# Expert visits in two sizes: 18 of 256 rows and 51 of 384 instead of 65 of 384

## The chip, the core and the metric

The kernel runs on one core of a Trainium2 chip. The metric is the device time of one execution in microseconds (us), the median over several runs. The core's engines are PE (matrix multiply, with its weight loads, PEld), DVE (vector), ACT (scalar activation), POOL (GpSimd) and SP, which only issues DMAs here.

## The reference

Three stages follow one another on 8 x 3072 = 24576 rows of 256 numbers:

```python
X = np.fft.rfft(x, axis=1)                       # a filter in the frequency domain
x = np.fft.irfft(X * F, n=3072, axis=1).reshape(24576, 256)

expert_idx = argmax(normalised(x) @ normalised(expert_emb).T / tau)   # 8 experts
for e in range(8):                               # each row goes to one expert
    mask = expert_idx == e
    out[mask] = gate_w[mask, None] * (np.maximum(x[mask] @ w1[e], 0) @ w2[e])
    # w1[e]: 256 x 1024, w2[e]: 1024 x 256

h = x @ w_in                                     # w_in: 256 x 2048, given as float64
return (h - np.tanh(h)) @ w_out                  # w_out: 2048 x 256, float64
```

## The kernel before

**Three stages.** `fft_phase` transforms the rows, picks an expert for each and scatters the row (with its gate and its number) into that expert's part of `region` in DRAM. `Moe` then works through the experts in *visits*: a visit takes a fixed number of rows of one expert, multiplies by w1, applies relu, multiplies by w2 and stores the columns to `x2T`. `ff_phase` does the last stage on 48 tiles of 512 rows.

**Three products for one.** For accuracy each float32 operand is held as a high and a low part (`w1h`, `w1l`, `yh`, `yl`, `hh`, `hl`, `w2h`, `w2l`), and each product is three matmuls: high x high, high x low, low x high.

**Visits.** The first KV = 9 visits (256 rows each, TE) belong to one expert, chosen early, and run under the end of the first stage. After them stand 65 visits of TV = 384 rows. Their number is fixed when the kernel is built, so that it suffices for any split of the rows over the experts: 58 whole pieces and 7 that the experts' remainders may add. Which expert and which rows a visit takes is worked out on the chip, by `moe_schedule` (some 40 tiny DVE operations on one small table); SP reads expert, row and target column of each visit from this table. A visit beyond the last one that is needed does its work on columns that nobody reads. Visits go through the experts from the last to the first, so the weights change only where the expert does; the load of a visit's weights (`raw`, 4 DMAs of 512 KB, `wload`) is conditional on that. The splitting of weights into high and low parts (`split`) is done for every visit.

**The order inside a visit.** A visit has four steps, b2 = 0 to 3. The order in which each engine gets its work is written out by hand in the loop of `visits` (lines 882 to 908): in step (v, b2) come `up(v, b2)` (12 matmuls, L807), a quarter of the weight split of visit v + 1 (`w1l` on DVE in steps 0 and 1, `w2l` on POOL in steps 2 and 3, L757), one of three parts of preparing the rows of visit v + 1 (`scale` in step 0: `ys` on POOL L769, `it` on DVE L773; `turn` in step 1: transposes L778, L779; `parts` in step 2: `yh` on ACT, `yl` on DVE L786), `relu(v, b2)` (`hh` on ACT L817, `hl` on DVE L818), the load of the weights and, in step 2, of the rows of visit v + 2, then perhaps a piece of *side work*, and `down` of two steps earlier (12 matmuls, L835). At the end of a visit's last `down`, `finish` copies the output and takes its maximum (`mx`, DVE L846). So step (v, 1) holds the `mx` of visit v - 1.

**Side work.** `ff_weights` is a generator that turns the float64 weights of the last stage into float32 parts, on 32 blocks. Each block is three pieces of small integer operations on DVE: piece 1 (six operations, L469 to L474), piece 2 (four, L476 to L479), piece 3 (four, L481 to L485). `next(self.side)` emits one piece at its place in the order. Before, it is called in step 3 of every one of the 65 visits, and in step 1 of the first 36:

```python
if v >= KV and (b2 == 3 or b2 == 1 and v - KV < 100 - (NV - KV - 1)):   # L900
    next(self.side, None)
```

**Buffers.** `up` writes two PSUM tiles in a 384-row visit, from two pools that alternate by step; each pool has two tiles, so `up` of a step needs the `relu` of two steps earlier to be done.

Of the kernel before, what the change touches and what calls it, by code (L numbers as in the profile page):

```python
# [16 lines left out]
F32 = mybir.dt.float32  # L17
# [9 lines left out]
D = 256  # L27
# [92 lines left out]
def fft_phase(tc, K, x, fr, fn, fi, emb, tau, region, base, NB, CAP, moe):  # L120
# [3 lines left out]
    with ExitStack() as es:  # L124
# [51 lines left out]
        first = cp.tile([128, 8], F32, name="first")  # L176
        nc.vector.tensor_scalar(first, dec, -float(CAP), 8.0 * CAP + TV, op0=ALU.mult, op1=ALU.add)
        nc.vector.tensor_copy(base, first)
# [213 lines left out]
        def at(slot, f, *args):  # L392
            slots[slot].append(lambda: f(*args))
# [138 lines left out]

def moe_schedule(tc, cp, cnt, done, numbers, CAP, step):

    nc = tc.nc
    v = nc.vector
    A = lambda n: cp.tile([128, 8], F32, name=n)
# [8 lines left out]
    assert TV == 3 * 128 and CAP < 250 * 128  # L552
    v.tensor_scalar(t, left, 127.0, None, op0=ALU.add)
    v.tensor_copy(ti, t)
    v.tensor_scalar(ti, ti, 7, None, op0=ALU.logical_shift_right)
    v.tensor_copy(t, ti)
    v.tensor_scalar(t, t, 2.0, 171.0, op0=ALU.add, op1=ALU.mult)
    v.tensor_copy(ti, t)
    v.tensor_scalar(ti, ti, 9, None, op0=ALU.logical_shift_right)
    nv = A("scnv")  # L560
    v.tensor_copy(nv, ti)
    step()

    vin, sin = A("scvi"), A("scsi")
    v.tensor_tensor_scan(vin, ones, nv, 0.0, op0=ALU.mult, op1=ALU.add)
    v.tensor_tensor_scan(sin, ones, left, 0.0, op0=ALU.mult, op1=ALU.add)
    vis, e8 = numbers
# [4 lines left out]
    v.scalar_tensor_tensor(w, vis, -1.0, vin[:, 7:8], op0=ALU.mult, op1=ALU.add)  # L572
    v.tensor_scalar(wp, w, 0.0, None, op0=ALU.add)
    v.tensor_scalar(w, w, -1.0, None, op0=ALU.add)
# [9 lines left out]
    e, ep = expert(w, "a"), expert(wp, "b")  # L584
    step()
# [9 lines left out]
    ve, se, ne = pick(vin, "v"), pick(sin, "s"), pick(cnt, "n")  # L595
    step()

    j = col("scj")
    v.tensor_tensor(j, ve, w, op=ALU.subtract)
    v.tensor_scalar(j, j, -float(TV), None, op0=ALU.mult)  # L600
# [5 lines left out]
    v.scalar_tensor_tensor(row, row, float(TV), used, op0=ALU.add, op1=ALU.mult)  # L606
    v.tensor_tensor(dst, se, j, op=ALU.add)
    v.scalar_tensor_tensor(dst, dst, float(TV), used, op0=ALU.add, op1=ALU.mult)
    step()
    v.tensor_copy(res[:, 2:3], e)  # L610
    v.tensor_tensor(new, e, ep, op=ALU.not_equal)
    start = col("sclt")
    v.tensor_scalar(start, vis, 1.0, None, op0=ALU.is_lt)
    v.tensor_tensor(new, new, start, op=ALU.max)
    v.tensor_copy(resi, res)
    return resi


class Moe:
# [4 lines left out]


    def __init__(self, tc, gp, region, w1, w2, x2T, ids, N, CAP):
        self.tc, self.gp, self.region, self.w1, self.w2 = tc, gp, region, w1, w2
        self.x2T, self.ids, self.N, self.CAP = x2T, ids, N, CAP
        self.KV = (N - 2 * S) // (8 * TE)
        self.NV = self.KV + (N - self.KV * TE) // TV + 7  # L630
        self.mx = gp.tile([128, self.NV], F32, name="mx")
        self.sent, self.early = [], []
        self.sc = self.side = self.raw = None
        self.n = 0
        self.es = ExitStack()
# [74 lines left out]
    def visits(self):  # L710
        tc, region, x2T, ids, mx = self.tc, self.region, self.x2T, self.ids, self.mx
        N, CAP, KV, NV = self.N, self.CAP, self.KV, self.NV
# [77 lines left out]
        def up(v, b2):  # L790

            w1h, w1l = W[v][:2]
            yh, yl, _ = X[v]
            if v < KV:
                t = self.hp[0].tile([128, 2, TE], F32, name="h")
                h = [t[:, 0], t[:, 1]]
                H[v, b2] = [t]
            else:
                k = 4 * (v - KV) + b2
                h = [self.hp[k % 2].tile([128, 512], F32, name="h")[:, :TV] for j in range(2)]  # L800
                H[v, b2] = h
# [19 lines left out]
        def down(v, b2):  # L821
            w2h, w2l = W[v][2:]
            hh, hl = H.pop((v, b2))
            if b2 == 0:
                if v < KV:
                    t = self.op[0].tile([128, 512], F32, name="o")
                    O[v] = [t[:, :TE], t[:, TE:]]
                else:
                    O[v] = [self.op[(2 * (v - KV) + d + 1) % 4 > 0].tile([128, 512], F32, name="o")[:, :TV] for d in range(2)]
            for j in range(2):  # L830
                fb = 2 * b2 + j
                for d in range(2):
                    c = slice(128 * d, 128 * d + 128)
                    for n, (p, q) in enumerate(((w2h, hh), (w2h, hl), (w2l, hh))):
                        nc.tensor.matmul(O[v][d], p[:, fb, c], q[:, j], start=fb == 0 and n == 0 and (d == 0 or v >= KV),  # L835
                                         stop=fb == 7 and n == 2 and (d == 1 or v >= KV))
            if b2 == 3:
                finish(v)

        def finish(v):  # L840
# [41 lines left out]
        for k in range(len(steps) + LAG):  # L882
            if k < len(steps):
# [27 lines left out]
def ff_load(tc, pool, bufs, eng, x2T, ids, c):  # L911
# [7 lines left out]
    def load():  # L919
        return (eng.dma_start(x, x2T[:, TV:][:, c].rearrange("(k p) n -> p k n", p=128)),  # L920
                eng.dma_start(ix, ids[TV:][c].rearrange("(a p) -> p a", a=4)))

# [170 lines left out]
def build(tc, a, out, NB):  # L1093
    nc = tc.nc
    N = NB * S
    CAP = N + TV
    with ExitStack() as es:
# [4 lines left out]
        region = dp.tile([8 * CAP, 264], F32, name="region")  # L1102
        x2T = dp.tile([D, N + TV], F32, name="x2T")
        ids = dp.tile([N + TV], I32, name="ids")
        moe = Moe(tc, gp, region, a["w1"], a["w2"], x2T, ids, N, CAP)
        with tc.manual_schedule():
            fft_phase(tc, a, a["x"], a["fr"], a["fn"], a["fi"], a["emb"], a["tau"], region, cnt, NB, CAP, moe)
            sc = moe_schedule(tc, gp, cnt, moe.done, numbers, CAP, moe.step)
            wp = es.enter_context(tc.tile_pool(name="w", bufs=1, side="right"))
# [53 lines left out]
```

## Time and profile before

| | |
|---|---|
| median of 3 runs | 4018.46 us (4014.62 to 4025.91) |
| the profiled execution | 4024.83 us, span 4023.0 us |
| PE busy | 3904.8 us, 97% of the span |
| DVE, ACT, POOL busy | 65%, 62%, 51% |
| first matmul of the experts' stage, last | 590.7, 1815.6 us (its last `mx` at 1823.2) |
| granted clock of PE, mean | 0.99 |

The span runs from the first to the last instruction of the profiled execution. The first 590 us are the first stage, 733 to 1823 us the 65 visits, and what follows is the last stage. Busy shares are means over all of it; what counts for a stage is read in that stage.

### The profile page before, as it was taken

To read this page: it belongs to the slowest core of one execution; us is meant where nothing else is said; L and a number is where in the kernel's file an instruction comes from. 1 tells how busy PE (TensorE), PEld (TensorE's weight loads), DVE (VectorE), ACT (ScalarE), POOL (GpSimd) and SP (SyncE) were. 2 spreads that over 40 slices of the span, in tenths; PEclk is the share of its full clock that TensorE was granted. 3 is DMA by queue.
4 is the path that set the end of the run, shared out by engine and by line. 5 is a ranking of instruction groups with operands and counts; after the bars stand their busy time and mean duration, and the time that the engine had idled before them with its cause. 6 is when DMAs were issued, how large, how long until landed. Compare 5 with 4: busy or idle time off the path is not lost.

```text
span 4023.0 us, 65752 instructions
## 1 busy us (share of the span) xinstructions
PE 3904.8 (97%) x23204; PEld 3527.1 (88%) x23204; DVE 2621.8 (65%) x4370; ACT 2514.1 (62%) x4318; POOL 2051.7 (51%) x1514
## 2 busy tenths in 40 slices
PE   6899979999999999999999999999999999999998
PEld 3666659999999999999999999999999999999987
DVE  4799986788888877865555555555555555555554
ACT  3455544555555555556777777777777777777775
POOL 2366664344444444444555555555555555555545
PEclk8999999999999999999999999999999999999999
DMA  9898863332333232221000000000001000000000
GB/s 275 264 295 279 270 186 102 76 80 62 77 80 80 55 75 75 54 71 35 22 26 28 22 22 23 26 27 22 22 24 30 22 22 22 26 28 22 22 17 17
DMA packets 297874, 300.13 MB, mean 75 GB/s; under 512 B 158905, under 2 KB 240450, under 8 KB 297538
## 3 DMA queue, kind: packets, MB, share of 16 engines
q1 hardware_dynamic: 275714, 241.83, 21.3%
q0 software_dynamic: 18432, 51.14, 3.5%
q8 instruction: 184, 3.01, 0.3%
q10 hardware_dynamic: 3392, 2.90, 0.2%
q14 instruction: 152, 1.25, 0.1%
HBM read 282.46 MB, written 132.72 MB: 103 GB/s over the span
## 4 chain that ended last, share of the span: by engine, by line
PE 85%; DVE 7%; DMA 4%; issue 2%; POOL 1%; SPq 1%; ACT 1%; POOLq 0%; DVEq 0%; ACTq 0%
PE po L1034 27%; PE h L991 26%; PE h L807 14%; PE o L835 14%; DVE u L261 1%; DVE v L260 1%; DVE v L259 1%; DMA out<-ob,ix 1%; PE z L254 1%; PE z L269 1%; PE z L296 1%; PE L L308 1%; PE z L229 1%; DMA region<-Y,pi 1%; DMA z1d<-a 1%
## 5 line engine op out<-in xcount | busy, mean ns | idle before, releaser
L999 POOL TENSOR_TENSOR gl<-g,gh 128x512 fp32r<-128x512 f32 x768 | 992.9, 1293 | 987.7 <-ACT gh L998 980.4
L1008 DVE SCALAR_TENSOR_TENSOR s<-s,u 128x512 f32<-128x512 f32 x768 | 535.0, 697 | 951.9 <-ACT s L1007 950.1
L1034 PE MATMUL po<-wo,gh 128*128 128x256 f32 x6144 | 1143.0, 282 | 0.0
L1034 PEld LDWEIGHTS po<-wo,gh 128*128 128x128 f32 x6144 | 1007.3, 189 | 71.3
L1034 PE MATMUL po<-wo,gl 128*128 128x256 f32 x3072 | 874.7, 285 | 4.0 <-POOL gl L999 4.0
L1006 ACT ACTIVATE u<-h 128x512 f32<-128x512 f32 x768 | 459.0, 598 | 584.1 <-PE h L991 583.9
L991 PE MATMUL h<-xh,wih 128*128 128x512 f32 x1536 | 610.7, 398 | 0.1
L991 PE MATMUL h<-xl,wih 128*128 128x512 f32 x1536 | 607.6, 396 | 0.0
L991 PE MATMUL h<-xh,wil 128*128 128x512 f32 x1536 | 603.9, 393 | 0.0
L1034 PEld LDWEIGHTS po<-wo,gl 128*128 128x128 f32 x3072 | 581.2, 189 | 4.3 <-POOL gl L999 4.2
L1009 DVE TENSOR_TENSOR g<-s,h 128x512 f32<-128x512 f32 x768 | 529.1, 689 | 84.5 <-POOL gl L999 3.7
L1007 ACT ACTIVATE s<-u,beta 128x512 f32<-128x512 f32 x768 | 554.7, 722 | 25.2
L757 POOL TENSOR_TENSOR w2l<-raw,w2h 128x1024 fp32r<-128x1024 f32 x130 | 349.9, 2692 | 416.7 <-ACT w2h L756 414.4
L817 ACT ACTIVATE hh<-h 128x384 fp32r<-128x384 f32 (+1 forms) x556 | 269.5, 498 | 458.1 <-PE h L807 443.4
L998 ACT ACTIVATE gh<-g 128x512 fp32r<-128x512 f32 x768 | 485.4, 632 | 11.2 <-PE po L1034 4.9
L807 PE MATMUL h<-yh,w1h 128*128 128x384 f32 (+1 forms) x1184 | 392.4, 331 | 10.7 <-DVE hl L818 7.3
L807 PE MATMUL h<-yh,w1l 128*128 128x384 f32 (+1 forms) x1184 | 389.5, 329 | 2.4 <-DVE w1l L757 2.3
L807 PE MATMUL h<-yl,w1h 128*128 128x384 f32 (+1 forms) x1184 | 389.4, 329 | 0.1
L835 PE MATMUL o<-hh,w2h 128*128 128x384 f32 (+1 forms) x1184 | 388.4, 328 | 0.2 <-ACT x L845 0.2
L835 PE MATMUL o<-hl,w2h 128*128 128x384 f32 (+1 forms) x1184 | 388.2, 328 | 0.0
L835 PE MATMUL o<-hh,w2l 128*128 128x384 f32 (+1 forms) x1184 | 388.1, 328 | 0.0
L991 PEld LDWEIGHTS h<-xh,wil 128*128 128x128 f32 x1536 | 288.5, 188 | 71.0
(199 smaller groups left out, 6102.2 us busy)
## 6 DMA issues: line engine op xcount, KB each, us to landing
raw<-in_w SPq DMA_DIRECT2D x260, 512.0 KB
y<-region SPq DMA_DIRECT2D x260, 99.0 KB
x2T<-x SPq DMA_DIRECT2D x65, 384.0 KB
xt<-in_x SPq DMA_DIRECT2D x48, 512.0 KB
z1d<-a SPq DMA_DIRECT2D x96, 256.0 KB
A<-z1d SPq DMA_DIRECT2D x64, 384.0 KB
z3d<-b SPq DMA_DIRECT2D x128, 192.0 KB
bt<-z3d SPq DMA_DIRECT2D x96, 256.0 KB
```

The costliest lines, as they stand in the source:

```text
L757: eng.tensor_tensor(l, r, h.bitcast(F32), op=ALU.subtract)
L807: nc.tensor.matmul(h[j], p[:, k, c], q[:, k], start=n == 0, stop=n == 5)
L817: nc.scalar.activation(oh, t, AF.Relu)
L835: nc.tensor.matmul(O[v][d], p[:, fb, c], q[:, j], start=fb == 0 and n == 0 and (d == 0 or v >= KV), stop=fb == 7 and n == 2 and (d == 1 or ...
L991: nc.tensor.matmul(h, a[:, k, c], b[:, k], start=n == 0, stop=n == 5)
L998: nc.scalar.activation(gh, g, AF.Copy)
L999: nc.gpsimd.tensor_tensor(gl, g, gh.bitcast(F32), op=ALU.subtract)
L1006: nc.scalar.activation(u, h, AF.Square)
L1007: nc.scalar.activation(s, u, AF.Square, bias=beta)
L1008: nc.vector.scalar_tensor_tensor(s, s, KAPPA, u, op0=ALU.add, op1=ALU.mult)
L1009: nc.vector.tensor_tensor(g, s, h, op=ALU.mult)
L1034: nc.tensor.matmul(po[a // 2][:, a % 2], p[:, a], wo[:, f, q], start=f == 0 and n == 0 and a % 2 == 0, stop=f == 15 and n == 2 and a % 2 == 1)
```

## The change

The visits after the first nine come in two sizes. `moe_visits` sets their numbers: 9, then 18 of 256 rows, then 51 of 384 (for 24576 rows). `KF` = 27 is the first visit of 384. `moe_schedule` hands out whole pieces of 384 first, up to 51 in all, and lets the visits of 256 take what the experts then have left; the visits of 256 run first, from the last expert to the first, then the visits of 384 do the same again. In the first visit of each kind the weights are loaded in any case. The table costs 17 DVE operations more.

A visit of 256 rows is built like one of the first nine: one PSUM tile holds both halves of `up`, and `relu` is one operation on ACT and one on DVE for each step. It alternates between the two pools, so that four steps' tiles exist. Its weights are loaded and split like those of a visit of 384.

No side work is called in the visits of 256. In the visits of 384 it is called in steps 1 and 3, in step 2 too where v is no multiple of 3, and in all four steps of the first one. The spare columns and rows at the edges of `region` and `x2T` shrink from 384 to 256, so that 16 blocks of zeros are written instead of 24.

```diff
+def moe_visits(N):
+    first = (N - 2 * S) // (8 * TE)
+    rest = N - first * TE
+    full = -(-(rest - 8 * (TV - 1)) // TV)
+    return first, (rest - full * TV - 8) // TE + 8, full
...
-        self.KV = (N - 2 * S) // (8 * TE)
-        self.NV = self.KV + (N - self.KV * TE) // TV + 7
+        self.KV, few, full = moe_visits(N)
+        self.KF = self.KV + few
+        self.NV = self.KF + full
...
-        size = lambda v: TE if v < KV else TV
+        size = lambda v: TE if v < KF else TV
...
-            if v < KV:
-                t = self.hp[0].tile([128, 2, TE], F32, name="h")
+            k = 4 * (v - KV) + b2
+            if v < KF:
+                t = self.hp[k % 2 if v >= KV else 0].tile([128, 512], F32, name="h").rearrange("p (j n) -> p j n", j=2)
...
-                if v >= KV and (b2 == 3 or b2 == 1 and v - KV < 100 - (NV - KV - 1)):
+                if v >= KF and (b2 % 2 or v == KF or b2 == 2 and v % 3):
                     next(self.side, None)
...
 def moe_schedule(...):
+    vf, cut = A("scvf"), A("scct")
+    v.tensor_tensor_scan(vf, ones, nf, 0.0, op0=ALU.mult, op1=ALU.add)
+    v.tensor_scalar(vf, vf, float(NF), None, op0=ALU.min)
...
+    v.tensor_tensor(t, left, cut, op=ALU.subtract)
+    v.tensor_scalar(t, t, TE - 1.0, None, op0=ALU.add)
+    v.tensor_copy(ti, t)
+    v.tensor_scalar(ti, ti, 8, None, op0=ALU.logical_shift_right)
...
-        for i in range(TV // 128 * E):
-            at(31 + i, zeros, *divmod(128 * i, TV))
+        for i in range(TE // 128 * E):
+            at(31 + i, zeros, *divmod(128 * i, TE))
```

**Where the order moves.** The rows are an engine's instructions in program order: line, operation, output <- inputs, size.

DVE in the middle of a visit of 384, from step 2 of one visit to step 0 of the next; `cvm`, `cvl`, `cvr`, `cvf`, `wil` are the side work. Before:

```order
L786 TENSOR_TENSOR yl<-yt,yh 128x768
L818 SCALAR_TENSOR_TENSOR hl<-h,hh 128x384 x4
L476 TENSOR_SCALAR cvm<-cvs 128x256
L477 TENSOR_SCALAR cvl<-cvs 128x256
L478 TENSOR_TENSOR cvm<-cvm,cvl 128x256
L479 TENSOR_TENSOR cvf<-cva,cvm 128x256
L757 TENSOR_TENSOR w1l<-raw_5497,w1h 128x1024
```

The same place in the change, in a visit with side work in steps 1, 2 and 3:

```order
L823 TENSOR_TENSOR yl<-yt,yh 128x768
L855 SCALAR_TENSOR_TENSOR hl<-h,hh 128x384 x2
L476 TENSOR_SCALAR cvm<-cvs 128x256
L477 TENSOR_SCALAR cvl<-cvs 128x256
L478 TENSOR_TENSOR cvm<-cvm,cvl 128x256
L479 TENSOR_TENSOR cvf<-cva,cvm 128x256
L855 SCALAR_TENSOR_TENSOR hl<-h,hh 128x384 x2
L481 TENSOR_SCALAR cvl<-cvs 128x256
L482 SCALAR_TENSOR_TENSOR cvr<-cvl,cva 128x256
L484 TENSOR_TENSOR cvl<-cvf,wih 128x256
L485 TENSOR_TENSOR wil<-cvl,cvr 128x256
L794 TENSOR_TENSOR w1l<-raw_5489,w1h 128x1024
```

A second piece stands between the `hl` of step 2 and that of step 3; the one behind step 3 stays.

DVE in one visit after the first nine. Before, from the `mx` of a visit's step 1 to the `hl` of the next visit's step 0:

```order
L846 TENSOR_REDUCE mx<-x_7437 128x1
L786 TENSOR_TENSOR yl<-yt,yh 128x768
L818 SCALAR_TENSOR_TENSOR hl<-h,hh 128x384 x4
L469 TENSOR_SCALAR cva<-cvs 128x256
L470 TENSOR_SCALAR cva<-cva 128x256
L471 TENSOR_SCALAR cva<-cva 128x256
L472 TENSOR_SCALAR cva<-cva 128x256
L473 TENSOR_SCALAR cvm<-cvs 128x256
L474 TENSOR_TENSOR cva<-cva,cvm 128x256
L757 TENSOR_TENSOR w1l<-raw_5497,w1h 128x1024
L772 MEMSET it 32x32
L773 COPY it<-y 32x12
```

The same stretch of a visit of 256 in the change, and on to its next `hl`:

```order
L883 TENSOR_REDUCE mx<-x_7447 128x1
L823 TENSOR_TENSOR yl<-yt,yh 128x512
L855 SCALAR_TENSOR_TENSOR hl<-h,hh 128x2x256 x2
L794 TENSOR_TENSOR w1l<-raw_5489,w1h 128x1024
L809 MEMSET it 32x32
L810 COPY it<-y 32x8
L855 SCALAR_TENSOR_TENSOR hl<-h,hh 128x2x256
```

One `hl` stands where two stood, and there is no side work.

## Rows read from the trace of the kernel before

**Rows 1.** The page's chain of work that ended last, shares of the span by line.

```profile
PE po L1034 27%; PE h L991 26%; PE h L807 14%; PE o L835 14%; DVE u L261 1%; DVE v L260 1%; DVE v L259 1%; DMA out<-ob,ix 1%; PE z L254 1%; PE z L269 1%; PE z L296 1%; PE L L308 1%; PE z L229 1%; DMA region<-Y,pi 1%; DMA z1d<-a 1%
```

**Rows 2.** Windows of the experts' stage: length, then busy us (x instructions).

```profile
core 0: us, PE busy (x) PEld busy (x) DVE busy (x) ACT busy (x) POOL busy (x), PEclk, DMA share, GB/s
...
800.00:900.00 100.00, 98.21 (x567) 97.89 (x566) 87.50 (x150) 56.03 (x94) 44.62 (x18) 1.00 0.31 81
900.00:1000.00 100.00, 100.00 (x579) 100.00 (x578) 89.81 (x151) 56.75 (x95) 44.21 (x19) 1.00 0.23 60
...
1400.00:1500.00 100.00, 100.00 (x579) 100.00 (x578) 78.57 (x125) 56.10 (x92) 44.74 (x19) 1.00 0.31 76
```

**Rows 3.** The chain in order of time: start us, us, what; 690 to 760.

```profile
693.12 1.44 PE h L807 x12
...
741.01 2.08 PE h L807 x12
```

**Rows 4.** Timeline of DVE, one visit: start, us, line, operation, shapes [idle before <-releaser].

```profile
940.86 2.53 DVE L786 TENSOR_TENSOR yl<-yt,yh 128x768 fp32r<-128x768 f32 x1 [0.69 <-ACT yh L785]
943.31 1.68 DVE L818 SCALAR_TENSOR_TENSOR hl<-h,hh 128x384 fp32r<-128x384 f32 x3
...
945.89 0.28 DVE L469 TENSOR_SCALAR cva<-cvs 128x256 int32<-128x256 int32 x1
...
947.74 2.53 DVE L757 TENSOR_TENSOR w1l<-raw,w1h 128x1024 fp32r<-128x1024 f32 x1
...
951.35 1.20 DVE L757 TENSOR_TENSOR w1l<-raw,w1h 128x1024 fp32r<-128x1024 f32 x1
...
954.37 0.27 DVE L476 TENSOR_SCALAR cvm<-cvs 128x256 int32<-128x256 int32 x1
...
955.34 0.43 DVE L479 TENSOR_TENSOR cvf<-cva,cvm 128x256 int32<-128x256 int32 x1
...
957.50 2.54 DVE L786 TENSOR_TENSOR yl<-yt,yh 128x768 fp32r<-128x768 f32 x1 [0.73 <-ACT yh L785]
```

**Rows 5.** Timeline of POOL in the same visit.

```profile
940.17 5.48 POOL L757 TENSOR_TENSOR w2l<-raw,w2h 128x1024 fp32r<-128x1024 f32 x2 [7.04 <-ACT w2h L756]
947.71 1.47 POOL L769 TENSOR_TENSOR ys<-y 128x768 f32<-128x768 f32 x1 [2.06 <-DMA y<-region]
956.81 5.48 POOL L757 TENSOR_TENSOR w2l<-raw,w2h 128x1024 fp32r<-128x1024 f32 x2 [7.62 <-ACT w2h L756]
```

**Rows 6.** Timeline of DVE behind a reload of weights, 863 to 880.

```profile
866.22 0.16 DVE L773 COPY it<-y 32x12 int32<-32x12 int32 x1 [2.72 <-DMA y<-region]
...
871.70 2.37 DVE L469 TENSOR_SCALAR cva<-cvs 128x256 int32<-128x256 int32 x1
874.11 2.40 DVE L470 TENSOR_SCALAR cva<-cva 128x256 int32<-128x256 int32 x1
```

**Rows 7.** Timeline of POOL around the same reload.

```profile
854.88 5.48 POOL L757 TENSOR_TENSOR w2l<-raw,w2h 128x1024 fp32r<-128x1024 f32 x2 [6.51 <-ACT w2h L756]
867.85 1.93 POOL L769 TENSOR_TENSOR ys<-y 128x768 f32<-128x768 f32 x1 [7.48 <-DMA y<-region]
871.52 4.84 POOL L757 TENSOR_TENSOR w2l<-raw,w2h 128x1024 fp32r<-128x1024 f32 x2 [1.75 <-ACT w2h L756]
```

**Rows 8.** Timeline of PE, all matmuls from 735 us on with idle before.

```profile
880.08 0.44 PE L807 MATMUL h<-yh,w1h 128*128 128x384 f32 x1 [1.79 <-DVE hl L818]
...
1032.24 0.54 PE L807 MATMUL h<-yh,w1h 128*128 128x384 f32 x1 [2.10 <-DVE hl L818]
...
1168.23 0.44 PE L807 MATMUL h<-yh,w1h 128*128 128x384 f32 x1 [1.03 <-DVE hl L818]
...
1335.64 0.44 PE L807 MATMUL h<-yh,w1h 128*128 128x384 f32 x1 [0.72 <-DVE hl L818]
```

**Rows 9.** The chain in order of time, behind two of these stalls.

```profile
880.08 2.37 PE h L807 x12
...
1032.24 3.91 PE h L807 x12
```

**Rows 10.** Timeline of DVE: one operation of the schedule's table.

```profile
687.01 0.17 DVE L555 TENSOR_SCALAR scti<-scti 128x8 int32<-128x8 int32 x1
```

More of the change, by code (lines that the diff above doesn't have):

```diff
@@ L176, in fft_phase @@
         first = cp.tile([128, 8], F32, name="first")
-        nc.vector.tensor_scalar(first, dec, -float(CAP), 8.0 * CAP + TV, op0=ALU.mult, op1=ALU.add)
+        nc.vector.tensor_scalar(first, dec, -float(CAP), 8.0 * CAP + TE, op0=ALU.mult, op1=ALU.add)
         nc.vector.tensor_copy(base, first)
@@ L530, in moe_numbers, with moe_schedule @@
     return r
-def moe_schedule(tc, cp, cnt, done, numbers, CAP, step):
+def moe_visits(N):
[3 more added lines that the diff above has]
+    return first, (rest - full * TV - 8) // TE + 8, full
+def moe_schedule(tc, cp, cnt, done, numbers, N, CAP, step):
     nc = tc.nc
     v = nc.vector
+    _, NE, NF = moe_visits(N)
     A = lambda n: cp.tile([128, 8], F32, name=n)
@@ L550, in moe_schedule @@
     v.tensor_tensor(left, cnt, done, op=ALU.subtract)
-    assert TV == 3 * 128 and CAP < 250 * 128
-    v.tensor_scalar(t, left, 127.0, None, op0=ALU.add)
-    v.tensor_copy(ti, t)
+    vis, e8 = numbers
+    isf, is0 = col("scif"), col("sci0")
+    v.tensor_scalar(isf, vis, float(NE), None, op0=ALU.is_ge)
+    v.tensor_scalar(is0, vis, float(NE), None, op0=ALU.is_equal)
+    start = col("sclt")
+    v.tensor_scalar(start, vis, 1.0, is0, op0=ALU.is_lt, op1=ALU.add)
+    assert TV == 3 * 128 and TE == 2 * 128 and CAP < 250 * 128
+    v.tensor_copy(ti, left)
     v.tensor_scalar(ti, ti, 7, None, op0=ALU.logical_shift_right)
     v.tensor_copy(t, ti)
-    v.tensor_scalar(t, t, 2.0, 171.0, op0=ALU.add, op1=ALU.mult)
+    v.tensor_scalar(t, t, 171.0, None, op0=ALU.mult)
     v.tensor_copy(ti, t)
     v.tensor_scalar(ti, ti, 9, None, op0=ALU.logical_shift_right)
-    nv = A("scnv")
-    v.tensor_copy(nv, ti)
+    nf = A("scnf")
+    v.tensor_copy(nf, ti)
     step()
-    vin, sin = A("scvi"), A("scsi")
-    v.tensor_tensor_scan(vin, ones, nv, 0.0, op0=ALU.mult, op1=ALU.add)
+    vf, cut = A("scvf"), A("scct")
+    v.tensor_tensor_scan(vf, ones, nf, 0.0, op0=ALU.mult, op1=ALU.add)
+    v.tensor_scalar(vf, vf, float(NF), None, op0=ALU.min)
+    v.tensor_copy(cut, vf)
+    v.tensor_tensor(cut[:, 1:], vf[:, 1:], vf[:, :7], op=ALU.subtract)
+    v.tensor_scalar(cut, cut, float(TV), None, op0=ALU.mult)
+    v.tensor_tensor(t, left, cut, op=ALU.subtract)
+    v.tensor_scalar(t, t, TE - 1.0, None, op0=ALU.add)
+    v.tensor_copy(ti, t)
+    v.tensor_scalar(ti, ti, 8, None, op0=ALU.logical_shift_right)
+    v.tensor_copy(t, ti)
+    step()
+    vin, sin, ve_ = A("scvi"), A("scsi"), A("scve")
+    v.tensor_tensor_scan(ve_, ones, t, 0.0, op0=ALU.mult, op1=ALU.add)
     v.tensor_tensor_scan(sin, ones, left, 0.0, op0=ALU.mult, op1=ALU.add)
-    vis, e8 = numbers
+    v.tensor_tensor(t, vf, ve_, op=ALU.subtract)
+    v.scalar_tensor_tensor(vin, t, isf, ve_, op0=ALU.mult, op1=ALU.add)
     res = cp.tile([128, 4], F32, name="scres")
@@ L571, in moe_schedule @@
     w, wp = col("scw"), col("scwp")
[L572 to L574 removed]
+    v.scalar_tensor_tensor(wp, isf, float(NE), vis, op0=ALU.mult, op1=ALU.subtract)
+    v.tensor_tensor(wp, wp, vin[:, 7:8], op=ALU.add)
+    v.tensor_scalar(w, wp, -1.0, None, op0=ALU.add)
     def expert(x, nm):
@@ L584, in moe_schedule @@
     e, ep = expert(w, "a"), expert(wp, "b")
+    nend, send, nif = A("scne"), A("scse"), col("scni")
+    v.tensor_scalar(nif, isf, -1.0, None, op0=ALU.add)
+    v.scalar_tensor_tensor(nend, cut, nif, cnt, op0=ALU.mult, op1=ALU.add)
+    v.scalar_tensor_tensor(send, cut, nif, sin, op0=ALU.mult, op1=ALU.add)
     step()
@@ L593, in pick @@
         return r
-    ve, se, ne = pick(vin, "v"), pick(sin, "s"), pick(cnt, "n")
+    ve, se, ne = pick(vin, "v"), pick(send, "s"), pick(nend, "n")
     step()
-    j = col("scj")
+    j, size = col("scj"), col("scz")
     v.tensor_tensor(j, ve, w, op=ALU.subtract)
-    v.tensor_scalar(j, j, -float(TV), None, op0=ALU.mult)
+    v.tensor_scalar(size, isf, float(TE - TV), -float(TE), op0=ALU.mult, op1=ALU.add)
+    v.tensor_tensor(j, j, size, op=ALU.mult)
     used = col("scu")
@@ L605, in moe_schedule @@
     v.tensor_tensor(row, row, ne, op=ALU.add)
-    v.scalar_tensor_tensor(row, row, float(TV), used, op0=ALU.add, op1=ALU.mult)
+    v.scalar_tensor_tensor(row, row, float(TE), used, op0=ALU.add, op1=ALU.mult)
     v.tensor_tensor(dst, se, j, op=ALU.add)
-    v.scalar_tensor_tensor(dst, dst, float(TV), used, op0=ALU.add, op1=ALU.mult)
+    v.scalar_tensor_tensor(dst, dst, float(TE), used, op0=ALU.add, op1=ALU.mult)
     step()
@@ L824, in down @@
             if b2 == 0:
-                if v < KV:
-                    t = self.op[0].tile([128, 512], F32, name="o")
+                if v < KF:
+                    t = self.op[v >= KV].tile([128, 512], F32, name="o")
                     O[v] = [t[:, :TE], t[:, TE:]]
                 else:
-                    O[v] = [self.op[(2 * (v - KV) + d + 1) % 4 > 0].tile([128, 512], F32, name="o")[:, :TV] for d in range(2)]
+                    O[v] = [self.op[(2 * (v - KF) + d + 1) % 4 > 0].tile([128, 512], F32, name="o")[:, :TV] for d in range(2)]
             for j in range(2):
@@ L834, in down @@
                     for n, (p, q) in enumerate(((w2h, hh), (w2h, hl), (w2l, hh))):
-                        nc.tensor.matmul(O[v][d], p[:, fb, c], q[:, j], start=fb == 0 and n == 0 and (d == 0 or v >= KV),
-                                         stop=fb == 7 and n == 2 and (d == 1 or v >= KV))
+                        nc.tensor.matmul(O[v][d], p[:, fb, c], q[:, j], start=fb == 0 and n == 0 and (d == 0 or v >= KF),
+                                         stop=fb == 7 and n == 2 and (d == 1 or v >= KF))
             if b2 == 3:
@@ L1095, in build @@
     N = NB * S
-    CAP = N + TV
+    CAP = N + TE
     with ExitStack() as es:
@@ L1107, in build @@
             fft_phase(tc, a, a["x"], a["fr"], a["fn"], a["fi"], a["emb"], a["tau"], region, cnt, NB, CAP, moe)
-            sc = moe_schedule(tc, gp, cnt, moe.done, numbers, CAP, moe.step)
+            sc = moe_schedule(tc, gp, cnt, moe.done, numbers, N, CAP, moe.step)
             wp = es.enter_context(tc.tile_pool(name="w", bufs=1, side="right"))
```

17 lines of the change are left out of this document (7 added, 10 removed).

## The prediction

> **What bounds the kernel now.** I read first the chain that ended last [rows 1]: matmuls of the last stage (53%) and of the experts' visits (28%) make up most of it, so a change in the visits counts where it shortens PE's work or makes PE wait. Then the windows [rows 2]: among the visits PE is busy all the time at full clock in most of them, DVE 88 to 90% of the time in the first 36 visits (two pieces of side work each) and 79% later (one piece). So PE is the bound there, with DVE close behind it. The chain in order of time gives PE's price [rows 3]: a step's 12 matmuls take 2.08 us with 384 rows and 1.44 us with 256. Last, the timelines of DVE and POOL in one visit [rows 4, 5], and in a visit behind a reload of weights [rows 6, 7], where PE waits for DVE [rows 8].
>
> **The change, part by part.**
>
> *PE's work.* A visit has 8 groups of 12 matmuls: 16.64 us for 384 rows (2.08 x 8), 11.52 us for 256 (1.44 x 8). Before 65 x 16.64 = 1081.6; now 51 x 16.64 + 18 x 11.52 = 848.6 + 207.4 = 1056.0. That is **-25.6 us**, if PE never waits more than before. A third fewer rows save less than a third of the time: 1.44 is 69% of 2.08.
>
> [...]
>
> *Reloads of weights.* From the reference's inputs I counted rows by expert: before, the weights change 7 times; now the small visits change expert 7 times (six of these changes from one visit to the next or the one after), the first full visit reloads, and the full ones change 7 times more. So 8 reloads are added, all at small visits. What one does: `ys` on POOL started 12.97 us behind the start of the `w2l` pair (867.85 - 854.88) [rows 7] instead of 7.54 (947.71 - 940.17) [rows 5], because the rows' DMA is queued with 2 MB of weights, and `it` on DVE waited until 866.22 [rows 6], with the `hl` of that step behind it. In a full visit this could be borne: `hl` of step 0 is done 11.2 us behind POOL's start (951.35 - 940.17 [rows 4, 5]), and PE wants it at 15.1 (6.77, worked out below, and four groups of 2.08). In a small visit its `down` comes nine groups of 1.44 behind the end of the last visit's `down`, that is some 11 us behind POOL's start, and `it` alone was 11.3 us behind it in rows 6 (866.22 - 854.88). Bounds: nothing (three of the seven reloads before left no stall [rows 8]) and 3.9 us (the worst: 2.10 of waiting, then 3.91 instead of 2.08 for the next 12 matmuls [rows 8, 9]). The average before was 5.6/7 = 0.8; since the slack is smaller I take 2.0, as at 1032 us without what followed: **+16 us**, from 0 to 31. The windows speak for a busy DMA too: with one reload the share in 100 us is 0.31 instead of 0.23 [rows 2], so a reload costs 8 us of all 16 engines, in a visit of 11.5.
>
> *Side work in three steps.* This decides the sign. The pieces are the same 32 x 3, but now none lies in the small visits, and two of three full visits carry three pieces until the generator is empty, some 36 visits on: 24 visits with three pieces. A piece is 1.4 us (954.37 to 955.77) to 1.85 us (945.89 to 947.74) [rows 4]. Busy time alone would allow it: 14.9 us a visit (0.89 x 16.64) plus 1.65. [...] When a piece began just behind the start of `w2l`, its first two operations took 2.37 and 2.40 us [rows 6] where 0.28 is normal [rows 4], one for each of POOL's two operations; `w1l` took 2.53 instead of 1.20 beside `ys` [rows 4, 5]. `hl`, which reads PSUM, is not held.
>
> Now the visit of rows 4 with a third piece. The `hl` pair of step 2 ends at 944.43 (second of three from 943.31). Before, the `hl` of step 3 followed. Now a piece does; POOL's second `w2l` runs to 945.65, so its first operation is held to there and the piece ends at 947.0. `hl` of step 3: 948.1. The piece of step 3 meets `ys` (to 949.2) and ends at 950.7, `w1l` 1.17 later, and from there the row's own steps follow: 1.14 us to the end of `hl` of step 0, 3.02 more to the piece of step 1. That begins at 956.0 instead of 954.37. POOL's next pair starts at 956.81, since ACT and PE are on time. Two or three of the piece's four to six operations fit ahead of it; the next two are held to 4.95 us behind POOL's start, then come the piece's last 0 to 0.4 us, `mx`, `yl` and the first `hl` (2.3 together): 7.2 to 7.6. PE needs this `hl` 6.77 us behind POOL's start (880.08 - 1.79 - 871.52 [rows 7, 8]). So PE waits some **0.9 us**, much like 1.03 and 0.72 [rows 8]. A second three-piece visit starts with `hl` about 4 us late in DVE's order. By the same count its step-1 piece begins 1 us behind POOL's start, all its operations but two run after the pair, and PE waits **1.5 us**, near the 1.79 of rows 8, where a piece began 0.18 us behind POOL's start [rows 6, 7]. A two-piece visit then recovers. 12 x 0.9 + 12 x 1.5 = 29; and the 12 matmuls behind a stall take 2.37 instead of 2.08 [rows 9], 24 x 0.29 = 7. Together **+36 us**. Bounds: nothing, if the pieces fit; 24 x 3.93 = 94, if each visit costs what 1032 us did (2.10 + 1.83, the clock having fallen).
>
> *The schedule.* 17 operations more at some 0.2 us from start to start (0.17 busy [rows 10]) are 3.4 us, partly in DVE's idle time between steps, ahead of the first scheduled visit's loads. Against it, that visit loads a third fewer rows. I take **+1**, from -2 to 3.4. Eight blocks of zeros less lie in the first stage beside a busy DMA: 0 to -2, taken as 0. Relu of small visits, more PSUM tiles, POOL's `w2l` in shorter visits (5.48 + about 1 of 11.5 us): beside PE, 0; were POOL's cover gone, `hl` of step 2 would be next, as above.
>
> **The sum.** -25.6 + 16 + 36 + 1 = +27. Against the profiled execution's 4024.8 that is 4052; this execution was 6.4 above the median of the runs, 4018.5, so I forecast **4046 us**.
>
> **The rivals.**
>
> *The pieces fit.* The step-1 piece would have to begin 0.6 to 1.0 us sooner than I count. That is less than the 1.2 us for which I hold the first operation of the new piece; if POOL's second `w2l` doesn't hold it, all three pieces end ahead of POOL's pair and PE doesn't wait. For it: each hold is small against a visit, and before, no two-piece visit without a reload waited. Against: rows 6 show just such operations held. Then -25.6 + 16 + 1 = -9: **4010 us**.
>
> *Faster.* The same, and the rows arrive in time in the small visits as in three of the seven reloads before: the point from which it decides is that `it` of a small visit lies no more than some 2 us later than in rows 4. Then PE's saving stands alone, -25.6 + 1: **3994 us**. Against it: six reloads almost in a row, each with 8 us of DMA.
>
> *The clock falls as well.* Short stalls, repeated, drop the granted clock as at 1032 us. Halfway from my 36 to the bound of 94 is 65: -25.6 + 16 + 65 + 1 = +56, **4075 us**.
>
> That the change doesn't do what it says can be left out: the number of visits stands in the program's order.
>
> **How the numbers follow.** What a measurement of this kernel can tell from no change is about 0.3%, 12 us: 4006 to 4031. Forecast 0.52 (own range 4024 to 4068; 0.07 of it below 4031), pieces fit 0.22 (3998 to 4022; 0.09 faster, 0.13 same), faster 0.16, clock 0.10. So faster 0.25, same 0.20, slower 0.55. The range of 3995 to 4072 leaves out half of the fast case and most of the slow one, under 2 in 10.
>
> **What would show it.** Right: PE's idle list has about two entries of 0.5 to 2 us, released by `hl`, in every three full visits until some 36 full visits are done, and none after; DVE operations of the side work of 2.4 us there; the small visits' 18 taking 207 us plus some 16. The matmul groups still 1.44 and 2.08. Wrong: full visits at an even 16.64 us with three pieces (my count of holds is wrong), or small visits near 11.5 at reloads, or far above it (then DMA or SP sets their pace).

## The result, and the profile after

The change takes 4043.19 us, median of 4 runs (4041.53 to 4045.07), against 4016.63 for the kernel before on the same chip: a ratio of 1.0054, 95% interval 1.0042 to 1.0066. It is slower by 27 us by the two medians and by 22 by the ratio; the forecast was 4046, +27. The total is that of the forecast, but of its terms only PE's work is near what was measured. The errors of the others cancel, which is luck.

The profiled execution took 4041.53 us, span 4039.8. The span of before, 4023.0, belongs to an execution some 8 us over the median found here, so the two profiles lie only 16.8 us apart. The `mx` operations cut each span into parts (us, from the start of one `mx` to the start of another, worked out from the timelines of DVE; the rows for other kernels are used further down):

| | to the 9th `mx` | 18 small visits | full visits | from the last `mx` to the end |
|---|---|---|---|---|
| before | 737.6 | | 1085.7 (65) | 2199.8 |
| change | 724.3 | 260.5 | 876.3 (51) | 2178.7 |
| by the matmul prices of [rows 3] | | 207.4 | 848.6 (before: 1081.6) | |
| side work in two steps | 729.4 | 260.5 | 851.6 | 2178.7 |
| no reloads in small visits | 728.0 | 221.2 | 877.0 | 2180.1 |
| both of these (two_noreload) | 724.0 | 222.2 | 851.1 | 2180.2 |

So the visits cost 51.1 us more (260.5 + 876.3 - 1085.7), and the rest gives 34.4 back: 13.3 ahead of the visits and 21.1 in the last stage, where no instruction was changed.

The windows of the change, to be held against [rows 2]: length, busy us (x instructions) of PE, PEld, DVE, ACT, POOL, then granted clock, DMA share, GB/s.

```profile
724.00:793.00 69.00, 69.00 (x577) 68.95 (x576) 60.60 (x72) 43.29 (x66) 38.83 (x18) 1.00 0.21 49
793.00:960.00 167.00, 139.31 (x1067) 137.19 (x1066) 86.59 (x127) 78.76 (x120) 70.96 (x32) 0.92 0.48 132
...
985.00:1571.00 586.00, 559.55 (x3169) 551.38 (x3168) 548.02 (x944) 315.12 (x526) 215.82 (x99) 0.99 0.29 77
1571.00:1861.00 290.00, 288.48 (x1663) 288.08 (x1663) 208.68 (x299) 154.16 (x255) 111.22 (x49) 1.00 0.24 63
```

The first small visits keep PE busy; they belong to one expert. From 793 us on, where nearly each visit reloads, PE stands idle for 28 of 167 us, and DVE is busy only half of the time: it is not DVE's work that is late. From 985 to 1571 PE idles 26 us with DVE at 94%; once the side work is used up, almost nothing.

PE's idle list in the change answers to [rows 8]: start, us, operation, idle before and its releaser. The rows are examples of 11 such waits in the small visits (31.2 us), three of them 0.31 us long, and 22 in the full ones (27.9 us).

```profile
843.68 0.58 PE L872 MATMUL o<-hl,w2h 128*128 128x256 f32 x1 [4.77 <-DVE hl L855]
860.85 0.38 PE L872 MATMUL o<-hl,w2h 128*128 128x256 f32 x1 [3.05 <-DVE hl L855]
878.11 0.58 PE L872 MATMUL o<-hl,w2h 128*128 128x256 f32 x1 [4.85 <-DVE hl L855]
...
1148.53 0.44 PE L844 MATMUL h<-yh,w1h 128*128 128x384 f32 x1 [1.26 <-DVE hl L855]
...
1344.07 0.45 PE L844 MATMUL h<-yh,w1h 128*128 128x384 f32 x1 [0.93 <-DVE hl L855]
1362.80 0.45 PE L844 MATMUL h<-yh,w1h 128*128 128x384 f32 x1 [1.79 <-DVE hl L855]
...
1573.20 0.44 PE L844 MATMUL h<-yh,w1h 128*128 128x384 f32 x1 [1.52 <-DVE hl L855]
```

The first matmul behind the longest waits takes 0.58 us instead of 0.38. The mean granted clock of this stretch, 0.92, is a mix: it is 1.00 from 793 to 808 us and 0.50 from 843.7 to 847, behind the wait of 4.77. So the waits aren't all: between 793 and 960 us, PE is busy for 139.31/1067 = 131 ns a matmul where 1.44/12 = 120 is the price, 11 us in all. Away from waits, the chain in order of time still gives the prices of [rows 3]:

```profile
740.93 1.44 PE h L844 x12
...
1600.51 2.08 PE o L872 x12
```

**The reloads, one behind another.** DVE waits for the rows, and the `hl` that PE wants stands behind `it` (timeline of DVE, ahead of PE's wait at 843.68):

```profile
842.87 0.16 DVE L810 COPY it<-y 32x8 int32<-32x8 int32 x1 [7.21 <-DMA y<-region]
842.96 0.67 DVE L855 SCALAR_TENSOR_TENSOR hl<-h,hh 128x512 fp32r<-128x512 f32 x1
```

The chain that ended last in 826 to 846 us of the change: shares by line, then start, us, what.

```profile
by line: DMA y<-region 67.0%; POOL w2l L794 23.9%; SPq L763 23.0%; POOL ys L806 15.3%; issue 4.5%; SPq L694 2.4%; SPq L709 2.0%; POOLq L806 0.6%; POOLq L794 0.4%
...
828.44 2.42 POOL w2l L794
...
830.88 0.41 SPq L709
...
832.95 3.15 SPq L763
...
836.89 7.00 DMA y<-region
...
844.17 1.49 POOL ys L806
845.66 2.35 POOL w2l L794
```

This is a loop, with no matmul in it. SP's load of the third quarter of the weights (L709) needs `w2l` to have read the only `raw` buffer; the rows `y` stand behind that load in SP's order; their four issues take 5.2 us (832.02 to 837.2) and 7.0 more to land; then `ys`, and behind it on POOL the next `w2l`. Once round is 845.66 - 828.44 = 17.2 us, and six `mx` in a row here stand 16.8 to 17.6 us apart, where PE's work for a visit is 11.5.

**A visit with three pieces.** Timelines of DVE and POOL in the change, to be held against [rows 4, 5].

```profile
1141.82 1.25 DVE L476 TENSOR_SCALAR cvm<-cvs 128x256 int32<-128x256 int32 x1
1142.99 0.28 DVE L477 TENSOR_SCALAR cvl<-cvs 128x256 int32<-128x256 int32 x1
...
1143.77 2.51 DVE L479 TENSOR_TENSOR cvf<-cva,cvm 128x256 int32<-128x256 int32 x1
1146.20 0.94 DVE L883 TENSOR_REDUCE mx<-x 128x1 f32<-128x768 f32 x1
1147.07 0.94 DVE L823 TENSOR_TENSOR yl<-yt,yh 128x768 fp32r<-128x768 f32 x1
1147.93 1.94 DVE L855 SCALAR_TENSOR_TENSOR hl<-h,hh 128x384 fp32r<-128x384 f32 x4
```

```profile
1140.50 2.42 POOL L794 TENSOR_TENSOR w2l<-raw,w2h 128x1024 fp32r<-128x1024 f32 x1 [7.45 <-ACT w2h L793]
1143.56 2.44 POOL L794 TENSOR_TENSOR w2l<-raw,w2h 128x1024 fp32r<-128x1024 f32 x1 [0.64 <-ACT w2h L793]
```

The piece meets POOL's pair: its first operation ends with the first `w2l`, its last with the second (2.51 us instead of 0.43 [rows 4]). PE gets its `hl` at 1148.53, 8.03 us behind POOL's start, where the prediction had 6.77 as the latest: 1.26 late, the wait in PE's list. Not every operation of DVE loses time beside POOL. Between 735 and 1800 us of the change, `yl` 128x768 takes 2.53 us (median of 20) where it lies wholly beside POOL's work and 0.95 (median of 10) away from it, but the transpose `yt` 128x768 takes 0.98 (of 6) and 0.96 (of 40), `mx` of 128x768 0.94 (of 4) and 0.94 (of 32), and `hl` of 128x384 0.56 (of 7) and 0.56 (of 32).

### The profile page after: what moved, and what is told of

It reads as the page before. It is cut to its first block, busy times and chain, and to the rows that moved or that the text cites. A ratio compares the mean times of both kernels' runs of the same rounds, so it can differ in the third digit from the quotient of the medians.

```text
span 4039.8 us, 66772 instructions
## 1 busy us (share of the span) xinstructions
PE 3878.6 (96%) x23588; PEld 3487.4 (86%) x23588; DVE 2643.4 (65%) x4379; ACT 2494.0 (62%) x4306; POOL 2027.6 (50%) x1526
## 3 DMA queue, kind: packets, MB, share of 16 engines
q14 instruction: 154, 1.26, 0.1%
## 4 chain that ended last, share of the span: by engine, by line
PE 72%; DVE 14%; DMA 7%; issue 2%; SPq 2%; POOL 2%; ACT 1%; POOLq 0%; DVEq 0%; ACTq 0%
PE h L1028 26%; PE po L1071 26%; PE h L844 8%; PE o L872 8%; DMA y<-region 2%; DVE hl L855 2%; SPq L763 1%; DVE u L261 1%; DVE v L260 1%; DVE v L259 1%; DMA A<-z1d 1%; DMA out<-ob,ix 1%; DVE w1l L794 1%; PE z L254 1%; PE z L269 1%
## 5 line engine op out<-in xcount | busy, mean ns | idle before, releaser
L1071 PE MATMUL po<-wo,gh 128*128 128x256 f32 x6144 | 1118.4, 279 | 0.0
L1071 PEld LDWEIGHTS po<-wo,gh 128*128 128x128 f32 x6144 | 992.5, 188 | 69.2
L1071 PE MATMUL po<-wo,gl 128*128 128x256 f32 x3072 | 858.5, 279 | 3.4 <-POOL gl L1036 3.4
L854 ACT ACTIVATE hh<-h 128x384 fp32r<-128x384 f32 (+1 forms) x516 | 257.3, 511 | 363.9 <-PE h L844 358.6
L844 PE MATMUL h<-yh,w1h 128*128 128x384 f32 (+1 forms) x1248 | 404.8, 324 | 32.2 <-DVE hl L855 28.9
L872 PE MATMUL o<-hl,w2h 128*128 128x384 f32 (+1 forms) x1248 | 398.7, 319 | 31.3 <-DVE hl L855 31.2
L844 PE MATMUL h<-yh,w1l 128*128 128x384 f32 (+1 forms) x1248 | 399.5, 320 | 0.6 <-DVE w1l L794 0.5
L844 PE MATMUL h<-yl,w1h 128*128 128x384 f32 (+1 forms) x1248 | 399.5, 320 | 0.0
L872 PE MATMUL o<-hh,w2l 128*128 128x384 f32 (+1 forms) x1248 | 397.2, 318 | 0.0
L872 PE MATMUL o<-hh,w2h 128*128 128x384 f32 (+1 forms) x1248 | 397.2, 318 | 0.0
```

Of the source, the lines that this page charges most:

```text
L844: nc.tensor.matmul(h[j], p[:, k, c], q[:, k], start=n == 0, stop=n == 5)
L854: nc.scalar.activation(oh, t, AF.Relu)
L1071: nc.tensor.matmul(po[a // 2][:, a % 2], p[:, a], wo[:, f, q], start=f == 0 and n == 0 and a % 2 == 0, stop=f == 15 and n == 2 and a % 2 == 1)
```

## The experiments

Ratios are against the kernel before on the same chip; its medians there were 4027.2 us (beside two_pieces, no_reload, rows_first and both), 4021.4 (before_third, two_noreload, before_shift), 4021.1 (rows_act, after_even) and 4024.0 (before_pad8, before_pad80).

**Side work in two steps** (two_pieces). The third piece goes, the rest of the change stays.

```diff
-                if v >= KF and (b2 % 2 or v == KF or b2 == 2 and v % 3):
+                if v >= KF and (b2 % 2 or v == KF):
```

> The change with side work only in steps 1 and 3 of the full visits (and in all four of the first). If the third piece is what makes PE wait in the full visits: the 20 waits of the change between 986 and 1574 us (26 us together) shrink to the few that the reloads leave (about four, 5 us), and with the slower matmuls behind each stall some 25 us come off: about 4018 us, the small visits unchanged. If the waits in the full visits come from the reloads or from anything else: about 4040 us, the waits still there.

4023.99 us, ratio 0.9993 (0.9983 to 1.0002). Full visits fall from 876.3 to 851.6 us, by 24.7. PE's waits in them fall from 22 (27.9 us) to 8 (11.4 us), behind 1031 us only four are left, and the same window has PE busy for 576.1 instead of 559.6 us:

```profile
985.00:1571.00 586.00, 576.13 (x3312) 573.58 (x3311) 514.28 (x883) 324.95 (x541) 252.01 (x105) 1.00 0.30 77
```

The 16.5 us of waits aren't the whole 24.7. A matmul takes 576.13/3312 = 174.0 ns in this window and took 559.55/3169 = 176.6 in the change: 8 us more over the 3169, from the slower matmuls behind the waits.

**The third piece alone** (before_third): the kernel before, with pieces in steps 1 and 3 and in step 2 of two visits of three.

```diff
-                if v >= KV and (b2 == 3 or b2 == 1 and v - KV < 100 - (NV - KV - 1)):
+                if v >= KV and (b2 % 2 or b2 == 2 and v % 3):
```

> The kernel before with the side work's third piece alone: pieces in steps 1 and 3 of each scheduled visit, and in step 2 of two visits of three, nothing else changed. Theory (the third piece makes TensorE wait): its visits become 25 to 35 us longer than 1085.7 us, with waits of about 1.3 us behind hl that end once the side work is used up, and the ratio is 1.006 to 1.009. Rival (the third piece costs only where small visits have gone before it): visits within 5 us of 1085.7 us and a ratio within 0.002 of 1.

4055.95 us, ratio 1.0086 (1.0069 to 1.0102). The visits take 1118.8 us, 33.1 more than 1085.7, with 22 waits behind `hl` of 30.5 us in all (4 of 5.6 us before), the last at 1384 us, when the side work is used up. So the third piece costs this with no small visit near it.

**No reloads in the small visits** (no_reload). The table's flag for loading is multiplied by `isf`, so the small visits after the first compute with the weights that are there.

```diff
-    v.tensor_tensor(new, new, start, op=ALU.max)
+    v.scalar_tensor_tensor(new, new, isf, start, op0=ALU.mult, op1=ALU.max)
```

> The change without the weight loads inside the 18 small visits, except in the first (so their outputs are computed with another expert's weights); every instruction is still issued. If the rows' DMA queued behind the weights is what slows the small visits (270 us from the last early visit's maximum to the last small one's, instead of 18 x 11.52 = 207): they take about 210 us, and the time is about 3983 us. If the small visits are slow for another reason (DVE, POOL, SP's own work): still above 250 us, and about 4035 us.

4012.35 us, ratio 0.9968 (0.9959 to 0.9978). The small visits take 221.2 us, 39.3 less than 260.5 (the 270 of the expectation is too high), 5.6 for each of the seven reloads left out; the full ones 877.0, all but unchanged. Sixteen small visits now run at full clock without a gap, and what is over 207.4 lies at the last two (36.8 us), where the first full visit loads its weights in any case (915 to 950):

```profile
728.00:915.00 187.00, 187.00 (x1560) 186.95 (x1559) 161.43 (x194) 118.62 (x180) 108.57 (x49) 1.00 0.21 50
915.00:950.00 35.00, 31.10 (x212) 30.57 (x211) 24.05 (x33) 17.16 (x28) 16.23 (x8) 0.95 0.46 117
```

**Both of these** (two_noreload), the two edits together. Otherwise than its expectation says, the full visits load their weights as they do in the change, since `isf` is 1 there; only the small visits after the first don't.

> The changed kernel with both costs taken away: side work in steps 1 and 3 alone (and all of the first full visit), and no scheduled visit but the first of each size loads weights, so most visits compute with another expert's weights. Theory (the two costs are apart and add): small visits about 221 us and full ones about 851 us, 64 us less than the change, about 3.6 us under what two_pieces and no_reload would give one by one, a ratio near 0.990. Rival (the two share their waits, so that one without the other keeps part): no more than 45 us less than the change, a ratio of 0.994 or more.

3981.21 us, ratio 0.9901 (0.9885 to 0.9918): 222.2 and 851.1 us, 63.5 less than in the change, where the two savings one by one are 39.3 and 24.7. The two costs are apart and add.

**The rows ahead of the weights** (rows_first; with two steps of side work: both).

```diff
+                    if v + 2 > KV and b2 == 0:
+                        load(v + 2)
                     if v + 2 >= KV:
                         wload(v + 2, b2)
-                    if b2 == 2:
+                    if v + 2 <= KV and b2 == 2:
                         load(v + 2)
```

> The change with the load of the next rows moved from behind the third quarter of the weights (step 2) to ahead of the first one (step 0). If the rows' place in SP's queue closes the loop w2l - weights - rows - ys - w2l: the small visits come down from 270 to 215 to 230 us (the weights' own landing, for which ACT waits 50 us in all, may then be next), the full visits change by a few us at reloads, and the time is about 4000 us. If the DMA engines' time is the limit: no more than 10 us better, about 4035 us.

> Rows first and two pieces together. If both reasons hold and are apart from one another: the two savings add, about 3975 us, 1% under the kernel before. If either was an effect of the other: about what the better of the two gives alone, 4000 to 4015 us.

rows_first took 4060.76 us, 1.0087 (1.0071 to 1.0104); both 4019.67, 0.9981 (0.9971 to 0.9990). The small visits grew to 265.9 and 266.3 us. I missed here: the rows came in time (DVE no longer waits for them), but another loop took the place of the first. The full visits took 885.0 us in rows_first, longer than in the change, for a reason that isn't shown. In both they took 840.7, 10.9 less than in two_pieces, with one wait of 2.3 us left of eight: there the move does help. The chain of both in 836 to 876 us:

```profile
by line: DMA raw<-in_w 113.0%; issue 5.8%; ACT w1h L793 5.3%; DVE yt L815 1.2%; DVE w1l L794 0.2%
...
834.89 15.13 DMA raw<-in_w
...
850.04 1.07 ACT w1h L793
...
852.51 15.01 DMA raw<-in_w
```

`w1l` frees a quarter of `raw`, its load lands 15 us later, and only then can `w1h` begin: 17.6 us once round.

**The rows in a queue of their own** (rows_act, on top of two steps of side work): ACT issues the small visits' rows.

```diff
-                d = nc.sync.dma_start(y[32 * i : 32 * i + 32, : n // 32], rv[i])
+                d = (nc.scalar if KV + 1 < v < KF + 2 else nc.sync).dma_start(y[32 * i : 32 * i + 32, : n // 32], rv[i])
```

> The changed kernel with side work in steps 1 and 3 alone (as two_pieces) and with the rows of the small visits (and of the first two full ones) issued by ACT into a queue of its own, no longer behind the weights in SP's queue. Theory (the rows are late because they stand behind weights in one queue): the waits behind hl in the small visits go, these take about 222 us instead of 260.5, ACT's issues cost nothing on the path, and the time is some 38 us under that of two_pieces, a ratio near 0.990. Rival (the weights themselves, through one raw buffer, set the pace as in both): small visits 255 to 266 us and a ratio near 0.998. A third way: ACT loses some 2 us a visit to the issues and the small visits grow past 266 us.

4026.89 us, 1.0012 (1.0002 to 1.0022); small visits 273.0 us, past the rival's 266. The rival's loop is there, a little slower than in both (chain, 800 to 880 us):

```profile
808.37 15.53 DMA raw<-in_w
823.92 1.07 ACT w1h L793
825.02 1.24 DVE w1l L794
...
826.73 16.25 DMA raw<-in_w
```

But the third way came true as well, with more than 2 us: ACT is held by the four issues for 8.87 us, and PE waits for the `hh` behind them (timelines of ACT and PE).

```profile
828.58 8.87 ACTq L763 DMA_DIRECT2D y<-region  x4
839.10 0.58 PE L872 MATMUL o<-hh,w2h 128*128 128x256 f32 x1 [3.79 <-ACT hh L854]
```

So this run doesn't part the loop from the issues. What no_reload, rows_first and both show together is that the loads of the weights are the root, and that rows which come sooner don't cure it. Whether a second `raw` buffer or a faster load would wasn't tried; more on the load stands in the last section. With the rows issued by ACT, a landing of the weights still takes 15.5 to 16.3 us (rows above), against 15.0 to 15.1 in both.

**The addresses in the last stage.** The schedule has nine small tiles more than before, and the table `mx` 78 columns instead of 74, 16 bytes. By the expectation of before_shift, what is allocated behind them, the last stage's `gh`, `gl` and `xh` too, stands 288 bytes higher in SBUF. Four kernels move it by the length of `mx` alone; before_again is the kernel before, once more (a single run, 4017.54 us).

```diff
-        self.mx = gp.tile([128, self.NV], F32, name="mx")
+        self.mx = gp.tile([128, self.NV + 72], F32, name="mx")[:, : self.NV]
```

> The kernel before, unchanged, profiled once more. Theory (the place of the buffers sets the pace of the last stage): its last stage, from the last mx to the end, is again within 2 us of 2199.8 us, and the last mx stands again near 1085.7 us after the ninth. Rival (the 21 us by which the last stage differs is scatter between executions): the last stage falls anywhere from 2178 to 2200 us. The ninth mx again near 737.6 us would make the 13 us at the start the program's as well; near 725 us would make them scatter.

> The kernel before with its tile mx 72 columns longer (288 bytes per partition), so that the buffers gh, gl and those behind them stand at the addresses that they have in the changed kernel; no instruction differs. Theory (the addresses set the pace of the matmuls behind the gl ones in the last stage): the last stage falls from 2199.8 to about 2179 us and each such matmul from 126.7 to 116.7 ns, in all about 21 us less, a ratio near 0.995. Rival (something else of the change moves the last stage): 2199.8 us again and a ratio of 1.000.

> The changed kernel with its tile mx 8 columns (32 bytes per partition) longer, so that gh and gl begin at multiples of 64 bytes, as in the kernel before; no instruction differs. Theory (what counts is the address within 64 bytes): the last stage is 2200 us again instead of 2178.7 and the matmuls behind gl take 125 to 127 ns; the ratio is 1.0054 + 0.0053, some 1.0105, which is the change without the luck of its addresses. Rival (another granularity, or only the distance of 288 bytes): 2179 us again and a ratio of 1.005.

> The kernel before with mx 80 columns (320 bytes) longer, so that gh, gl and what lies behind them stand at the addresses of after_even; no instruction differs. Theory (the addresses alone set the pace of the last stage, whatever the visits are): last stage 2170 us as in after_even instead of 2199.8, some 30 us less, a ratio near 0.9927, less than both kernels. Rival (the 2170 of after_even belongs to its visits): 2179 us or more.

> The kernel before with mx 8 columns (32 bytes) longer. It stands at the same place within 128 bytes as the buffers 288 bytes higher (32), while 320 bytes higher is 64. Theory (the place within 128 bytes counts): last stage 2179 us as in before_shift, a ratio near 0.995. Rival (the distance itself, or a larger unit than 256 bytes, counts): near 2200 us and a ratio of 1.000.

| | moved by, bytes | of it over multiples of 128 | last stage, us | ratio |
|---|---|---|---|---|
| before, before_again | 0 | 0 | 2199.8, 2200.8 | |
| before_pad8 | 32 | 32 | 2178.8 | 0.9957 (0.9942 to 0.9972) |
| before_shift | 288 | 32 | 2179.2 | 0.9950 (0.9934 to 0.9967) |
| the change | 288 | 32 | 2178.7 | 1.0054 (1.0042 to 1.0066) |
| before_pad80 | 320 | 64 | 2169.9 | 0.9924 (0.9907 to 0.9942) |
| after_even | 320 | 64 | 2170.0 | 1.0038 (1.0026 to 1.0049) |

The last stage follows the shift alone, whatever visits went before it. My first unit, 64 bytes, was wrong (after_even should have gone back to 2200); a unit of 128 fits all, and so would 256. The chain in order of time shows where it lies, for before_again, before_shift and before_pad80 in this order:

```profile
2400.47 1.44 PE po L1034 x12
2401.91 1.40 PE h L991 x6
```

```profile
2401.67 1.41 PE po L1034 x12
...
2405.90 1.40 PE h L991 x6
```

```profile
2401.83 1.40 PE po L1034 x12
2403.23 1.40 PE h L991 x6
```

The matmuls that read `gh` and `gl` take 1.44, 1.41 or 1.40 us for 12. From start to start, the one behind a `gl` matmul comes after 123.9 ns on average in the kernel before and 117.7 in before_shift, not after the 126.7 and 116.7 of the expectation; other places among the 12 differ too. There are 768 such groups: 0.03 x 768 = 23 and 0.04 x 768 = 31 us, against 21 and 30 in the table. before_pad80, 3995.61 us, is thus faster than both kernels, with no instruction changed.

## Why the prediction came out

**PE's work**, -25.6: right. With both costs taken away the visits take 222.2 + 851.1 = 1073.3 us, 12.4 under 1085.7; of the missing 13 us most lies around the first full visit's reload, which these runs keep.

**Reloads of weights**, +16, from 0 to 31: the mechanism was right (the rows come late, `it` waits, `hl` is queued behind it), the size was wrong, outside the bounds too. The small visits took 53 us more than 207.4, and no_reload gives 39 of them back, for seven of the eight reloads. Of the 53, 31.2 are waits and more than 11 go to slow matmuls behind them. The step that failed is "I take 2.0": its price and both bounds came from reloads that stood alone, and the rows that I set beside it, 8 us of all DMA engines in a visit of 11.5, were read as a busy DMA and not as a loop. Behind one another the reloads make one, of 17.2 us, 5.7 more than a visit's matmuls.

**Side work in three steps**, +36: right in kind, place and size of a wait (0.9 and 1.5 predicted; 0.93 and 1.59 to 1.79 are common, none after 1574 us). Measured +24.7 by two_pieces, 33.1 in before_third. The 7 us for slow matmuls behind the waits are borne out: some 8 in either (in before_third the waits grew by 24.9 us, the visits by 33.1). What was too high for the change is the sum of the waits, 29 against 16.5. They are as long as forecast but fewer: between 1200 and 1525 us, some 19 visits, nine waits of 0.9 to 1.8 us stand where two in three visits would make 13. In before_third they come nearly as often as forecast; why they don't in the change isn't shown.

**The schedule and the start**, +1, taken with the zeros as nothing: the ninth `mx` came 13.3 us earlier. In six profiles of before and its variants it stands at 731 to 739 us (731.1 in before_again, between the two values of its expectation), in eight of the change and its variants at 721 to 733, so some 9 us by the means are the change's and the rest scatter. Which of its parts gives them wasn't tried.

**The last stage**, no term at all: -21.1, by an address. With the start, this is what made the total right, and nothing in the working foresaw it: against the spans, 51.1 for visits where I had 26.4 (-25.6 + 16 + 36), and -34.4 for what I had at +1. after_even and before_pad80 have one and the same shift and are the fairest pair: 4033.31 against 3995.61 us, the change is about 1% slower there (1.1% by the ratios, 1.0038/0.9924).

**The rivals.** "The pieces fit" and "faster" fell with the waits of 27.9 us. "The clock falls as well" came true mostly at another place: the granted clock falls to 0.50 five times between 808 and 969 us, among the reloads, and only twice among the full visits (0.50 from 1027 to 1029.5 and from 1170 to 1173 us, behind waits of 2.56 and 2.58 us). In the kernel before it was 0.50 from 1032.5 to 1035.8 us, behind the wait of 2.10. In before_third matmuls of 384 began 320 ns apart instead of 173 behind three of the four waits of 1.79 us.

## What to carry to other kernels

A price taken from an event that stands alone doesn't hold when the event comes every round: write down the loop (who frees the buffer, who is queued behind whom) and compare its length with the work it should hide behind. Two such loops can lie close together, 17.2 and 17.6 us here, and then curing the nearer shows only the next. And before a difference is explained by the edit, compare the stages that it doesn't touch: a few small tiles more, 288 bytes in all, moved 21 us in a stage that shares no instruction with them.

## What the runs showed of the hardware

The pace of the last stage's second product depended on where in SBUF the tiles behind `mx` begin: 1.44, 1.41 and 1.40 us for 12 matmuls at a shift of 0, 32 and 64 bytes over multiples of 128. `gh` and `gl` are the operand that is loaded as weights there, 128 x 128, while `wo` is the moving one of 256 columns (page of the kernel before):

```profile
L1034 PE MATMUL po<-wo,gh 128*128 128x256 f32 x6144 | 1143.0, 282 | 0.0
L1034 PEld LDWEIGHTS po<-wo,gh 128*128 128x128 f32 x6144 | 1007.3, 189 | 71.3
```

`xh` and `xl`, the moving operands of the first product, were shifted too, and its six matmuls take 1.40 us in all three. Which of the shifted tiles counts, and a shift of 96 bytes, weren't tried.

In rows_act, while w1's two quarters were on their way, the 16 DMA engines were about a quarter busy (windows below, columns as in the windows above); in the first stage of the change, from 100 to 150 us, they moved 317 GB/s with a share of 0.97.

```profile
835.00:840.00 5.00, 1.06 (x5) 0.57 (x4) 0.69 (x1) 2.50 (x4) 1.36 (x1) 0.85 0.31 100
840.00:843.00 3.00, 3.00 (x15) 3.00 (x16) 2.85 (x4) 0.48 (x1) 1.00 (x1) 0.50 0.26 94
```

A share of 0.25 is what 4 of 16 engines would make, and the outermost dimension of w1's load (L705) is 4. The trace of the run both shows four packets at once: in 834 to 850 us, w1's two quarters come as 256 packets of 4 KB (a row of w1 is 4 KB), 205 ns each; of the time in which any of them runs, four run at once for 76% and more for 6%. In the change it is alike: from 793 to 960 us, 2019 packets of 4 KB of 197 ns, four at once for 77% of the time and more for 7%. 256 x 205 / 4 is 13 us, most of the 15 that a landing takes. The packets of 1 KB, w2's among them (outermost dimension 128), run 12 or more at once for 30% of theirs. My estimate from these figures is that w1's packets, four at a time, make most of the 15 us. That it is the 4 in the load's shape that keeps them to four isn't shown: a load of w1 in another shape wasn't tried.

The second row also shows PE, after the wait of 3.79 us that ended at 839.10, at a granted clock of 0.50: from 840.2 us its matmuls of 256 take 0.41 us, where in the change they take 0.28 at 1.00 (from 826.7 us).
